# One block's signal transform with one split less, 32-row filter taps, a filter sum moved to transfers, and a new order of work

## The chip, the cores and the metric

The program runs on one core of one Trainium2 chip. The metric is device time in microseconds (us) of one execution, lower is better. The kernel before takes 259.0 us (median of three runs, 258.26 to 259.75).

The core has a matrix engine (TensorE, PE in the profile; PEld is its weight load), a vector engine (VectorE, DVE), an activation engine (ScalarE, ACT), a general engine (GpSimd, POOL) and a queue engine (SyncE, SP). They run at the same time and wait for each other through semaphores. Matrix results land in PSUM and are copied ("evicted") to SBUF by ScalarE or VectorE. Transfers are issued by SP, POOL and ACT.

## The reference, cut to what matters

```
def _A_ref(q, k, v, shift_k, ssm_k, ssm_D):        # S = 2048 tokens, D = 640
    k_shift = sum over t in 0..3 of k[s-t] * shift_k[:, t]     # per channel
    kv = k_shift * v
    y = causal convolution of kv with ssm_k along the tokens (by FFT of length 2S)
    return q * (y + kv * ssm_D)
def _B_ref(x, w_gate, w_up, w_down):               # F = 1728
    return (silu(x @ w_gate) * (x @ w_up)) @ w_down
h  = A_q + _A_ref(_layernorm(A_q), A_k, A_v, A_shift_k, A_ssm_k, A_ssm_D)
h2 = h + _B_ref(_layernorm(h), B_w_gate, B_w_up, B_w_down)
```

Everything is bfloat16 in and out.

## The kernel before, in words

The 2048 tokens are four blocks of 512, numbered 0 to 3; token 4p+j of a block lies in partition p, slot j. The long convolution is done block by block with a transform of 512 points and 256 complex frequencies, written as matrix products with cosine and sine tables (`tab`, `itab`). A block's spectrum has shape [4, 2, 640]: four groups of 64 (f), real and imaginary part, channels.

The work is a list of named tasks. A name is a kind and a block, then a part:

- `ktM.p`, `kteM.p`: transposes of filter block M on TensorE and their eviction. `kfM.fpc`, `kfeM.fpc`: filter transform by `halves` and the evictions (f half, p parity of the slots, c cosine or sine). `kbM`: its butterfly on VectorE, where `kb2.1` and `kb3.1` are accumulating transfers of POOL.
- `kcM`: sums of neighbouring filter spectra. C[1] = C[0] + R1 (`kc1`, VectorE, two halves), C[2] = R1 + K2r (`kc2.s`, one VectorE instruction on 5120 elements a partition, L687), C[3] = K2r + K3r (`kc3.0`, `kc3.1`, POOL transfers).
- `tpI.c`: the four-tap short filter of k as small matrix products with diagonal weights (L734), `keI.c` its eviction into XT (shared with the spectrum buffer XH of the same parity), `kvI.c` the product with v on VectorE (L745). Block 0 has its own path.
- `xfI`, `xfeI`, `xbI`: the signal transform, its evictions and butterflies. Block 0 uses `fulls` (groups of eight matmuls, no butterfly). `halves` splits once: eight groups of four matmuls, and two butterfly instructions of 2560 elements a partition. `quads` (set `R4X`) splits twice: eight groups of two matmuls (L622), then four butterflies of 1280 and two of 2560 (L637).
- `pJI`: product of signal spectrum J and filter spectrum C[I-J] into Y[I] (L780), in parts; those ending in `e` may be POOL accumulating transfers (L571). `p02.d` is block 2's first use of C[2], `p03` block 3's first use of C[3] and the last use of XH0.
- `ybI`, `ivI.j`: inverse butterflies and inverse transform (L922, L927). Each `ivI.j` is followed on ScalarE by an eviction `e`, a mean `m`, a square sum `s`, on VectorE by `g`, `v`, `n`, and on POOL by `r` (L840). The normalized rows go by a transposing transfer `htI.j` on SP into hnT.
- `fgI.hq`, `fuI.hq`: gate and up products of half h of the block's columns (L1032), 20 matmuls each (15 for q = 3, gate and up together). `sg`, `su`, `sv` evict them (`su` into the single buffer `ub`), `mu` multiplies (L1053). `dnI.j` is the down product (L1118; L995 for the last tile), `rsI.j` and `raI.j` add it to h (the latter an accumulating transfer), `outI.j` stores.
- `la`, `lp`: the first layer norm. `gdI.h` copies the last, half-filled gate row to the upper partitions.

Dependencies are found from the memory cells that tasks read and write, and from PSUM: the 8 banks are four units of two banks, each matmul group opens one unit, and the order plus the list `units` say which. What runs where and in which order is written out in `PLAN`: one list of task numbers for each engine. Nothing is reordered at run time: an engine that waits holds up all behind it, and so does a transfer queue that waits for its source.

Before, `KD = (3,)`, `R4X = (1,2,3)` and the taps work on 64 rows:

```
for c0 in (0, 2, 4):
    nc_ = min(2, NC5 - c0)
    pt = g.tile()
    ...
                for r in range(2):
                    rows = slice(64 * r, 64 * r + 64)
                    last = e.matmul(pt.f(r, 64 * (j1 - j0), o=256 * b + 64 * j0), ks[rows, c, k0:k0 + 509:4], ...
```

For each chunk of 128 channels that is seven shifts times two row groups of 64: 14 matmuls of 64, 128, 192 or 256 columns, 70 a block.

Of the kernel before, what the change touches and what calls it, by code (L numbers as in the profile page):

```python
# [1228 lines left out]
```

## Time and profile before

| what | value |
|---|---|
| time of the runs | 259.0 us median, 258.26 to 259.75 |
| profiled execution, its span | 256.0 us (the page gives no other time for it) |
| granted TensorE clock | 1.000 |
| matmuls | 2253 |
| TensorE / VectorE / ScalarE / GpSimd busy | 248.5 / 199.8 / 184.6 / 58.6 us |
| transfers | 35.29 MB, mean 138 GB/s |

The span is the time from the first to the last instruction. A busy time counts the span in which at least one instruction of the engine runs; matmuls overlap, so a matmul's own duration (0.27 to 0.30 us) is longer than the step from one to the next. The chain that ended last is followed back from the last instruction, at each step to what released it. Times of single tasks come from the timeline, in which each engine's instructions stand in the order of its `PLAN` list.

### The profile page before, as it was taken

How to read it: one execution, taken by the hardware profiler on the slowest of the kernel's cores; microseconds unless marked ns; L12 is line 12 of the kernel's file. 1: busy time of each engine (PE TensorE's matmuls, PEld its weight loads, DVE VectorE, ACT ScalarE, POOL GpSimd, SP SyncE). 2: the span in 40 equal slices, each digit the busy share in tenths (PEclk: the TensorE clock that was granted, in tenths of full speed). 3: DMA queues.
4: the chain of work that ended last, by engine and by line, in shares of the span. 5: the costliest groups of instructions: out<-in, count | busy, mean ns of one | idle time of the engine just before them, and what ended most of it. 6: DMA issues, size and time to landing. Idle time of an engine off the chain costs nothing.

```text
span 256.0 us, 5303 instructions
## 1 busy us (share of the span) xinstructions
PE 248.5 (97%) x2253; PEld 194.7 (76%) x2253; DVE 199.8 (78%) x256; ACT 184.6 (72%) x302; POOL 58.6 (23%) x56
## 2 busy tenths in 40 slices
PE   7999997999999999999999999999999999999995
PEld 4767773587888766888887766788886678888763
DVE  3698999999999999999999989999959534111142
ACT  2489999999996895587899789739981854526410
POOL 1001003082312053950030813334130314000000
PEclk9999999999999999999999999999999999999999
DMA  6999946787995049886956036497870142600011
GB/s 224 323 339 208 403 161 134 220 207 192 326 188 95 0 75 126 150 165 168 248 100 109 3 55 139 108 213 139 149 128 0 30 100 43 140 0 3 0 45 57
DMA packets 37620, 35.29 MB, mean 138 GB/s; under 512 B 21203, under 2 KB 32478, under 8 KB 37598
## 3 DMA queue, kind: packets, MB, share of 16 engines
q1 hardware_dynamic: 31792, 23.82, 33.2%
q0 software_dynamic: 5792, 11.14, 25.3%
q8 instruction: 17, 0.28, 0.4%
q14 instruction: 5, 0.04, 0.1%
q10 hardware_dynamic: 14, 0.01, 0.0%
HBM read 16.55 MB, written 2.62 MB: 75 GB/s over the span
## 4 chain that ended last, share of the span: by engine, by line
PE 59%; DVE 32%; DMA 4%; POOL 1%; SPq 1%; issue 1%; ACT 0%; DVEq 0%
PE ps L1032 32%; PE ps L1118 16%; DVE tt L780 9%; DVE Y L780 5%; DMA tab<-cst_tab 4%; PE ps L602 3%; PE ps L922 2%; DVE gu L1053 2%; DVE C L780 2%; DVE XH L637 2%; DVE C L564 2%; PE ps L995 2%; PE ps L622 2%; PE ps L584 2%; POOL mv L840 1%; SPq L450 1%
## 5 line engine op out<-in xcount | busy, mean ns | idle before, releaser
L1118 PE MATMUL ps<-Wd,gu 128*128 128x320 bf16 (+1 forms) x420 | 58.7, 300 | 0.0
L1118 PEld LDWEIGHTS ps<-Wd,gu 128*128 128x128 bf16 (+1 forms) x420 | 38.7, 97 | 18.4 <-issue 3.6
L780 DVE TENSOR_TENSOR tt<-XH,C 128x2560 bf16<-128x2560 bf16 (+1 forms) x31 | 47.8, 1572 | 0.6 <-ACT XH L458 0.6
L1053 DVE TENSOR_TENSOR gu<-gu,ub 128x1024 bf16<-128x1024 bf16 (+1 forms) x32 | 19.9, 621 | 26.4 <-ACT gu L1040 13.8
L1040 ACT ACTIVATE gu<-ps 128x1024 bf16<-128x1024 f32 (+1 forms) x32 | 29.4, 924 | 12.1 <-PE ps L1032 11.9
L1045 ACT ACTIVATE ub<-ps 128x1024 bf16<-128x1024 f32 x24 | 24.6, 1024 | 13.3 <-PE ps L1032 11.4
L1032 PE MATMUL ps<-hnT,GB 128*128 128x256 bf16 x280 | 34.0, 273 | 0.0
L1032 PE MATMUL ps<-hnT,UB 128*128 128x256 bf16 x280 | 33.8, 273 | 0.0
L1032 PEld LDWEIGHTS ps<-hnT,UB 128*128 128x128 bf16 x280 | 27.3, 98 | 3.4 <-ACT KO L458 0.2
L1032 PEld LDWEIGHTS ps<-hnT,GB 128*128 128x128 bf16 x280 | 27.2, 98 | 3.3
L1032 PE MATMUL ps<-hnT,GA 128*128 128x256 bf16 x240 | 28.8, 273 | 0.0
L1032 PE MATMUL ps<-hnT,UA 128*128 128x256 bf16 x240 | 28.5, 273 | 0.1
L840 POOL TENSOR_TENSOR mv<-mv,half 128x1 f32<-128x1 f32 x16 | 21.2, 1328 | 23.9 <-DVE mv L838 23.9
L1032 PEld LDWEIGHTS ps<-hnT,UA 128*128 128x128 bf16 x240 | 23.4, 98 | 3.4 <-ACT C L458 0.5
L1032 PEld LDWEIGHTS ps<-hnT,GA 128*128 128x128 bf16 x240 | 23.4, 98 | 3.2 <-DVE XH L461 0.3
L843 ACT ACTIVATE qo<-xh 128x640 bf16<-128x640 bf16 x28 | 21.0, 750 | 5.8 <-DMA xh<-in_A_q_dram 3.3
L584 PE MATMUL ps<-KT,tab 128*128 128x320 bf16 x128 | 19.8, 300 | 1.8 <-ACT K3r L458 0.7
L937 ACT ACTIVATE qo<-ps,one,st 128x640 bf16<-128x640 f32 x16 | 13.7, 887 | 9.8 <-PE ps L922 9.0
L571 POOL DMA_DIRECT2D xh<-RB x12 | 10.7, 889 | 34.4 <-DVE RB L1135 23.0
L584 PEld LDWEIGHTS ps<-KT,tab 128*128 128x128 bf16 x128 | 11.4, 98 | 8.6 <-ACT K3r L458 1.6
L840 POOL TENSOR_TENSOR st<-st,half 128x4 f32<-128x4 f32 x4 | 8.0, 1988 | 33.3 <-DVE st L835 21.5
L458 ACT ACTIVATE XH<-ps 128x640 bf16<-128x640 f32 x19 | 13.3, 736 | 1.4 <-PE ps L622 0.7
(112 smaller groups left out, 384.3 us busy)
## 6 DMA issues: line engine op xcount, KB each, us to landing
C<-US POOLq DMA_DIRECT2D x6, 640.0 KB, 6.0
kc<-in_A_ssm_k_dram SPq DMA_DIRECT2D x4, 640.0 KB, 10.3
xh<-in_A_q_dram SPq DMA_DIRECT2D x4, 640.0 KB, 5.6
out_dram<-xh SPq DMA_DIRECT2D x15, 160.0 KB, 1.9
kvo<-in_A_v_dram SPq DMA_DIRECT2D x3, 640.0 KB, 4.5
xh<-RB POOLq DMA_DIRECT2D x12, 160.0 KB, 2.9
Wd<-in_B_w_down_dram SPq DMA_DIRECT2D x1, 1280.0 KB, 7.9
C<-K3r POOLq DMA_DIRECT2D x2, 640.0 KB, 8.0
```

Source lines behind the costliest of these rows:

```text
L458: return e.activation(out=dst[1], in_=src(), func=ACTF.Copy, scale=scale)
L571: return g.add(name, "pool", lambda e, n: e.dma_start(dst, src, accum_op=ALU.add, max_dma_last_dim=4096), ("acc", 2 * int(np.prod(dst.shap ...
L584: last = e.matmul(pt.f(c, W), tab[:, f, cs, j], src[:, j, c * W:(c + 1) * W], start=(j == js[0]), stop=(j == js[1]))
L780: g.add(nm, "dve", lambda e, n_: e.tensor_tensor(out=d, in0=a, in1=b, op=op), ("sb", n * D), r=[a, b], w=[d])
L840: g.add(name + "r", "pool", lambda e, n: e.tensor_tensor(out=dst, in0=tmp, in1=hf, op=ALU.pow), ("pp", 4), r=[tmp, half[:]], w=[dst])
L843: g.add(name + "m", "act", lambda e, n: e.activation(out=junk, in_=x, func=ACTF.Identity, scale=-1.0 / D, accum_out=sm), ("aa", D, 0), r=[ ...
L937: g.add(nm + "e", "act", lambda e, n, pt=pt, q2=q2, s=s, j=j: e.activation(out=q2, in_=pt.f2(W), func=ACTF.Identity, scale=s[:, 3, j:j + 1 ...
L1032: last = e.matmul(pt.f(q // 2, 256, o=256 * (q % 2)), w[:, c, f0:f0 + P], hnT[:, c, cols], start=(c == 0), stop=(c == NC5 - 1))
L1040: g.add("sg%d.%d%d" % (i, h, gp), "act", lambda e, n, pa=pa, gv=gv, nf=nf: e.activation(out=gv, in_=pa.f(0, 256 * nf).rearrange("p (f x) - ...
L1045: g.add("su%d.%d%d" % (i, h, gp), "act", lambda e, n, pb=pb: e.activation(out=ub[:].rearrange("p b x -> p (b x)"), in_=pb.f(0, 1024), func ...
L1053: g.add("mu%d.%d%d" % (i, h, gp), "dve", lambda e, n, gv=gv, ubv=ubv: e.tensor_tensor(out=gv, in0=gv, in1=ubv, op=ALU.mult), ("sb", 256 * ...
L1118: last = e.matmul(pt.f(c, W), gu[k, fb, col(i, j)], Wd[k, fb, c * W:(c + 1) * W], start=st, stop=sp)
```

## The change

Six things change in what is computed, and the order of everything.

1. `R4X` loses block 1: `xf1` is made by `halves` instead of `quads`. Eight groups of four matmuls stand for eight of two, and `xb1` has two butterflies of 2560 instead of four of 1280 and two of 2560.
2. The taps of blocks 1 to 3 take the first four channel chunks in one task on 32 rows a matmul: 112 matmuls of 32 to 128 columns instead of 56 of 64 to 256. The task opens two PSUM units at once and has two evictions (`a`, `b`) of 1024 elements and one kv product of 2048. The fifth chunk stays on 64 rows.
3. `KD` gets block 2: `kc2` is two accumulating transfers issued by POOL (`kc2.0`, `kc2.1`), each 640 KB, instead of one VectorE instruction.
4. A task may open several PSUM units (`opens` is a list), and waits for the last users of each.
5. `KO`, the odd half of a filter transform, becomes four names at the same address. `DV`, `BNT` and `KOT` are added and empty.
6. `PLAN` is new throughout, the PSUM units with it.

```
-    KD = (3,)
+    KD = (2,3)
...
+    T32 = ((0, 4, 32), (4, 1, 64))
...
-    R4X = (1,2,3)
+    R4X = (2,3)
...
-            for c0 in (0, 2, 4):
-                nc_ = min(2, NC5 - c0)
-                pt = g.tile()
+            for c0, nc_, rr in T32 if i in KVACT else ((0, 2, 64), (2, 2, 64), (4, 1, 64)):
+                nr = P // rr
+                pts = [g.tile() for _ in range(nr // 2)]
...
-                            for r in range(2):
-                                rows = slice(64 * r, 64 * r + 64)
-                                last = e.matmul(pt.f(r, 64 * (j1 - j0), o=256 * b + 64 * j0), ks[rows, c, k0:k0 + 509:4], diag[rows, c, j0 - s:j1 - s, :],
-                                                start=(s == 0), stop=(s == -3))
+                            for r in range(nr):
+                                rows = slice(rr * r, rr * r + rr)
+                                x0 = rr * r % 64
+                                last = e.matmul(pts[r // 2].f(r % 2, rr * (j1 - j0), o=4 * rr * b + rr * j0), ks[rows, c, k0:k0 + 509:4],
+                                                diag[rows, c, j0 - s:j1 - s, x0:x0 + rr], start=(s == 0), stop=(s == -3),
+                                                **({"tile_position": (rr * r, 0)} if rr < 64 else {}))
...
-            if t.opens is not None:
-                prev = last.get(t.opens.unit)
+            for pt in t.opens:
+                prev = last.get(pt.unit)
                 if prev is not None:
-                    t.pre = {x for x in prev.users if x.eng != "pe"}
-                    t.deps.update(t.pre)
-                last[t.opens.unit] = t.opens
+                    t.pre |= {x for x in prev.users if x.eng != "pe"}
+                last[pt.unit] = pt
+            t.deps.update(t.pre)
```

The new order, with task names for the numbers, over the stretch that the prediction speaks of. TensorE:

```
kt0.0 kt0.1 xf0.00 kf0.010 kf0.000 kf0.001 kf0.011 kf0.100 kf0.101 xf0.20 kf0.110 kf0.111 kt1.1 kt1.0 xf0.21 xf0.01
kt2.0 xf0.10 xf0.30 xf0.11 xf0.31 kf1(six) tp1.4 kf1.100 kf1.000 kt3.0 tp1.0 kt2.1 iv0.0 kf2.100 kf2.000 iv0.1
kf3.000 kf3.100 kt3.1 kf2.110 kf2.011 kf2.001 kf3.101 kf2.111 kf2.101 kf2.010 iv0.3 xf1.011 xf1.100 iv0.2 xf1.001
xf1.110 xf1.010 xf1.101 kf3.001 xf1.111 xf1.000 fg0.00 kf3.010 fg0.01 kf3.111 kf3.110 kf3.011 fu0.00 fu0.01 fu0.02
fg0.03 fg0.02 fu0.10 fg0.10 fg0.12 dn0.0 fg0.11 iv1.0 dn0.0b iv1.1 fu0.11 iv1.3 fu0.12 iv1.2 fg0.13 dn0.1 dn0.2
dn0.3 fg1.00 tp2.0 tp2.4 fu1.00 fg1.02 xf2.31 ... dn1.2 xf3.01 xf3.10 iv2.3 iv2.2 xf3.11 xf3.31 dn1.3 xf3.30 xf3.21
xf3.00 xf3.20 fu2.00 ...
```

It was, from the same point: `kt0.0 kt0.1 xf0.01 xf0.00 kf0(eight) kt1.1 kt1.0 xf0.20 xf0.21 kt2.0 xf0.31 kt2.1 xf0.11 xf0.10 xf0.30 kf1(seven) kt3.0 kf1.110 tp1.2 tp1.0 iv0.0 iv0.1 tp1.4 kf2.101 iv0.2 iv0.3 kf3.001 kf2.100 kf2.111 xf1.30 xf1.31 kf2.010 ... fu0.00 xf1.20 xf1.00 fg0.00 xf1.21 fg0.01 kt3.1 kf3.100 fu0.01 kf3(six) fu0.02 fg0.11 ... dn1.3 xf3(eight) fg2.00 ...`

VectorE, from the product of block 0 on:

```
p00(eight) kv1.4 yb0.0 kb1.0 kte2.1 kb1.1 iv0.0g yb0.1 kv1.0 kfe2.110 iv0.1g iv0.0v kte3.1 kfe2.001 kc1.s2 iv0.1v
iv0.0n kc1.s0 iv0.1n kb2.0 iv0.3g xfe1.001 iv0.2g p01.a p01.b iv0.2v xb1.0 iv0.3v p01.c iv0.2n p01.d iv0.3n kb3.0
xb1.1 mu0.00 p11.0(a b c d) mu0.01 p11.0e p11.1a mu0.02 p11.1(b c d) mu0.03 p11.1e la1v gd0.0 yb1.0 p02.d yb1.1
mu0.10 iv1.0g p02.a iv1.1g p02.c iv1.0v p02.b mu0.11 ... p03.a iv1.3n p03.c kv2.4 p03.d kv2.0 ... mu1.00
```

POOL: `... kb2.1 kc2.1 iv0.2r iv0.3r kb3.1 kc2.0 kc3.1 kc3.0 la1r ra0.0 ...` (before: `kb2.1 iv0.3r iv0.2r kb3.1 kc3.1 kc3.0 la1r p02.e ...`). SP, from the loads of block 1: `kT1 itab GB v1 PKu UA GA WdC UB x1 WdB kT2 ht0.0 ht0.1 WdA ht0.2 ht0.3 ht1.1 ...` (before: `kT1 GA itab UB v1 UA kT2 PKu ht0.0 ht0.1 GB WdC x1 WdB ht0.3 ht0.2 v2 WdA ht1.0 ...`). GA, GB, UA, UB and Wd are the FFN weights; WdA overwrites the space of the filter transposes KT and waits for the last `kf3`.

More of the change, by code (lines that the diff above doesn't have):

```diff
@@ L97, in add @@
         t.pre = set()
-        t.opens = None
+        t.opens = []
         t.tiles = []
@@ L118, in add @@
             if not pt.writers:
-                t.opens = pt
+                t.opens.append(pt)
             else:
@@ L217, in emit @@
                 wait_for(t, t.pre | {x for x in t.deps if x.name == fill[0]})
-                prog["pe"].append(lambda e, t=t, fill=fill: self.filler(e, t.opens, *fill))
+                prog["pe"].append(lambda e, t=t, fill=fill: self.filler(e, t.opens[0], *fill))
             wait_for(t, t.deps)
@@ L356, in bass_sequential_preLN__ssm_conv_h3__swiglu_ffn__prompt_kernel @@
     BN = (0,)
-    BNH = ()
+    BNT = ()
+    KOT = ()
     DT = ()
@@ L411, in bass_sequential_preLN__ssm_conv_h3__swiglu_ffn__prompt_kernel @@
         v0 = sb("v0", 134400, [4, D])
-        KO = sb("KO", 143616, [2, 2, D])
+        KO = [sb("KO%d" % m, 174336 if m in KOT else 143616, [2, 2, D]) for m in range(4)]
         ub = sb("ub", 148736, [2, N])
@@ L660, in kfwd @@
             if m in R4K:
[L661 removed]
+                quads("kf%d" % m, KT[m], dst, KO[m], D ** 0.5 / N, m)
                 return
@@ L731, in mm @@
                             k0 = 16 + s
[L732 to L738 removed]
+                            for r in range(nr):
[4 more added lines that the diff above has]
+                                                **({"tile_position": (rr * r, 0)} if rr < 64 else {}))
+                    return last
+                g.add("tp%d.%d" % (i, c0), "pe", mm, ("tap%d" % rr, nc_), r=[diag[:, c0:c0 + nc_], ks[:, c0:c0 + nc_, :]], pw=pts)
+                pt = pts[0]
                 cols = slice(c0 * P, (c0 + nc_) * P)
@@ L742, in taps @@
                     ks_ = XT[i % 2][:, c0:c0 + nc_, :]
-                    evac("ke%d.%d" % (i, c0), (ks_, ks_.rearrange("p b (r y) -> p r b y", r=2)),
-                         lambda pt=pt, nc_=nc_: pt.f2(256 * nc_).rearrange("p r (b y) -> p r b y", b=nc_), N * nc_, pt)
-                    g.add("kv%d.%d" % (i, c0), "dve", lambda e, n, d=d, vv=vv, ks_=ks_: e.tensor_tensor(
-                        out=d.rearrange("p j (b x) -> p b j x", x=64), in0=ks_.rearrange("p b (r j x) -> p (b r) j x", r=2, j=4),
-                        in1=vv.rearrange("p j (b x) -> p b j x", x=64), op=ALU.mult), ("sb", N * nc_), r=[vv, ks_], w=[d])
+                    kr = ks_.rearrange("p b (r y) -> p r b y", r=nr)
+                    for h, pt in enumerate(pts):
+                        kh_ = kr[:, 2 * h:2 * h + 2]
+                        evac("ke%d.%d%s" % (i, c0, "ab"[h] if nr > 2 else ""), (kh_, kh_),
+                             lambda pt=pt, nc_=nc_, rr=rr: pt.f2(4 * rr * nc_).rearrange("p r (b y) -> p r b y", b=nc_), 8 * rr * nc_, pt)
+                    g.add("kv%d.%d" % (i, c0), "dve", lambda e, n, d=d, vv=vv, ks_=ks_, rr=rr, nr=nr: e.tensor_tensor(
+                        out=d.rearrange("p j (b x) -> p b j x", x=rr), in0=ks_.rearrange("p b (r j x) -> p (b r) j x", r=nr, j=4),
+                        in1=vv.rearrange("p j (b x) -> p b j x", x=rr), op=ALU.mult), ("sb", N * nc_), r=[vv, ks_], w=[d])
                     continue
@@ L799, in prod @@
                 op2(nm + ".d", yim, u[:, :, 0], u[:, :, 1], ALU.add, 4)
+                return
+            if (j, i) in DV:
+                x, k, re = XH[j % 2][:], cm[:], tt[:, 1].rearrange("p a b d -> p (a b) d")
+                im = US[:].rearrange("p a b c d -> p (a b) c d")
+                ksw = bass.AP(k.tensor, k.offset + D, [list(k.ap[0]), [2 * D, 4], [-D, 2], [1, D]])
+                nm = "p%d%d" % (j, i)
+                for f2 in range(2):
+                    s = slice(f2, f2 + 3, 2)
+                    op2(nm + ".%da" % f2, t1, x[:, s], k[:, s], ALU.mult, 4)
+                    op2(nm + ".%dc" % f2, re[:, s], t1[:, :, odd], t1[:, :, 1 - odd], ALU.subtract, 2)
+                addto(nm + ".0e", y[:, :, odd], re)
+                op2(nm + ".0b", im, x, ksw, ALU.mult, 8)
+                for q in range(2):
+                    addto(nm + ".%df" % q, y[:, :, 1 - odd], im[:, :, q])
                 return
@@ L973, in inverse @@
                     stats(nm, x, q[:], m[:, 0:1], m[:, 1:2])
-                rstd(nm, m[:, 1:2], m[:, 3:4], m[:, 2:3], half[:, 0:1], i in BNH or i in SA, D ** -2.0 if i in SA else float(D))
+                rstd(nm, m[:, 1:2], m[:, 3:4], m[:, 2:3], half[:, 0:1], (i, j) in BNT or i in SA, D ** -2.0 if i in SA else float(D))
                 if i in NACT:
@@ L984, in inverse @@
                 g.add(nm + "n", "dve", lambda e, n, x=x, q=q, m=m, mm_=mm_: e.tensor_scalar(
-                    out=q[:], in0=x, scalar1=mm_, scalar2=m[:, 3:4], op0=ALU.subtract if i in BNH + SA else ALU.add, op1=ALU.mult),
+                    out=q[:], in0=x, scalar1=mm_, scalar2=m[:, 3:4], op0=ALU.subtract if (i, j) in BNT or i in SA else ALU.add, op1=ALU.mult),
                       ("ts", D), r=[x, mm_, m[:, 3:4]], w=[q[:]])
```

34 lines of the change are left out of this document (15 added, 19 removed), and 53 rows, old and new, of the table PLAN.

## The prediction

> **What bounds the kernel now.** I read the page first: the busy shares, then the chain that ended last.
>
> ```profile
> PE 248.5 (97%) x2253; PEld 194.7 (76%) x2253; DVE 199.8 (78%) x256; ACT 184.6 (72%) x302; POOL 58.6 (23%) x56
> PE 59%; DVE 32%; DMA 4%; POOL 1%; SPq 1%; issue 1%; ACT 0%; DVEq 0%
> ```
>
> TensorE is busy nearly throughout, but a third of the chain is VectorE. The chain in order of time shows where it changes hands; columns are start, length, work.
>
> ```profile
> 23.62 0.56 PE ps L550 x10
> 24.18 3.27 PE ps L602 x24
> 27.47 0.71 ACT XH L458
> 28.28 2.90 DVE tt L780 x2
> ...
> 62.53 2.74 DVE C L687
> ...
> 111.64 1.55 DVE kvo L745 x3
> 113.23 0.72 PE ps L622 x4
> 113.95 2.18 PE ps L1032 x20
> ...
> 149.79 3.77 PE ps L1118 x28
> ```
>
> TensorE sets the pace to 27.5, VectorE from 28.3 to 113.2, TensorE again to the end. Two rows give streaming rates: 2.18/20 = 0.109 us for a matmul of 256 columns, 3.77/28 = 0.135 for one of 320. The windows view of the middle stretch and of the one place in it where TensorE starves:
>
> ```profile
> 28.30:109.30 81.00, 78.92 (x720) 60.11 (x720) 79.98 (x84) 71.14 (x122) 26.51 (x19) 1.00 0.71 167
> 39.82:49.23 9.41, 7.33 (x44) 3.03 (x42) 9.03 (x12) 9.41 (x18) 2.38 (x2) 1.00 0.61 129
> ```
>
> Columns are window, length, then busy PE, PEld, DVE, ACT, POOL. VectorE works 79.98 of 81.00 us. In the second window 44 matmuls of at most 0.135 us are 5.9 us in 9.41: 3.5 us are lost, with ScalarE full (9.41 of 9.41). PSUM evictions hold TensorE there. Timelines of the two engines:
>
> ```profile
> 42.51 0.72 PE L584 MATMUL ps<-KT,tab 128*128 128x320 bf16 x4 [0.69 <-ACT K3r L458]
> 43.29 0.45 PE L622 MATMUL ps<-kvo,tab 128*128 128x320 bf16 x2
> 43.88 0.44 PE L622 MATMUL ps<-kvo,tab 128*128 128x320 bf16 x2
> 44.29 0.73 ACT L458 ACTIVATE XH<-ps 128x640 bf16<-128x640 f32 x1
> 44.87 0.74 ACT L458 ACTIVATE C<-ps 128x640 bf16<-128x640 f32 x1
> ```
>
> Block 1's transform gives two matmuls (0.27 us) per eviction, and starts follow the eviction pitch, 0.58 us.
>
> **The change, part by part.**
>
> *Block 1 split once.* Eight groups of two matmuls become eight of four: 16 x 0.135 = +2.15 us of TensorE. Evictions stay eight. In the starved stretch a group may last 0.58 us at no cost and four matmuls last 0.54, so I price it at 0 there. The cover is the 3.5 us; without it the cost is the whole 2.15. VectorE loses four butterflies of 1280; rows by line and shape:
>
> ```profile
> L637 DVE TENSOR_TENSOR OS<-XH,OS 128x1280 bf16<-128x1280 bf16 x6 | 4.9, 820 | 0.2 <-ACT OS L458 0.2
> L687 DVE TENSOR_TENSOR C<-C,C 128x5120 bf16<-128x5120 bf16 x1 | 2.8, 2822 | 0.0
> L461 DVE TENSOR_SCALAR KO<-ps 128x640 bf16<-128x640 f32 x1 | 0.8, 825 | 0.4 <-PE ps L584 0.4
> L460 DVE COPY KT<-ps 128x1280 bf16<-128x1280 bf16 x1 | 0.8, 815 | 0.0
> ```
>
> Instructions overlap by 0.08, as the chain's 2.74 for L687 against 2.82 shows, so four are 4 x 0.74 = -2.96 us.
>
> *Third filter sum by transfers.* kc2 leaves VectorE (L687): -2.74. Two accumulating transfers of 640 KB enter POOL's queue: kc2.1 ahead of iv0.2r, kc2.0 between kb3.1 and kc3.1. An issue takes 1.2 to 1.7 us there:
>
> ```profile
> 66.97 1.21 POOL L571 DMA_DIRECT2D K3r<-KO  x1 [7.55 <-DVE K3r L564]
> 67.72 1.69 POOL L571 DMA_DIRECT2D C<-K3r  x1
> 74.72 1.20 POOL L571 DMA_DIRECT2D C<-K3r  x1 [5.30 <-DMA K3r<-KO]
> 77.51 1.40 POOL L840 TENSOR_TENSOR st<-st,half 128x4 f32<-128x4 f32 x1 [1.60 <-DVE st L838]
> K3r<-KO POOLq DMA_DIRECT2D x1, 640.0 KB, 7.5
> C<-K3r POOLq DMA_DIRECT2D x1, 640.0 KB, 9.9
> ```
>
> Behind kc2.1 wait iv0.2r and iv0.3r, whose inputs come some 4 us later: nothing. Behind kc2.0 and kc3.0 waits la1r; it is needed by iv1.0's eviction near 81 and I expect it near 77: nothing, with 3 to 4 us of cover. Who waits for kc2.0 itself is p02.d on VectorE. Two accumulations together took 67.72 + 9.9 - 66.97 = 10.6 us, so three (kb3.1, kc2.0, kc3.1) should take about 16.0. From the end of kb3.0 to p02.d the new VectorE order has 16.7 us (one butterfly and yb1.0, 2.8; two half products and their adds, 11.4; four gate products and small ones, 2.5). That covers it by 0.7: cost 0, ends 0 and +4.
>
> *Evictions that change engine.* The new order gives VectorE kte2.1, kte3.1, kf2.110, kf2.001 and xf1.001 between 28 and 113: 5 x 0.74 = +3.7. ScalarE loses 3 x 0.58 and two copies of about 1.1: -4.0. That shortens the stretch where ScalarE is the limit.
>
> *Early order.* Before, TensorE idles 0.37 us for the second half of the transform table, and kt2.1 (0.56, the L550 row at 23.62) stands ahead of the last group that p00.1 needs. The new order runs four groups on the first half meanwhile and puts kt2.1 later: p00.1 starts 0.93 earlier than 28.28.
>
> *VectorE's sum to the end of block 2's kv products.* -2.96 - 2.74 + 3.7 = -2.0; gd0.0 moves here, +0.2; one kv product of 2048 for two of 1024, about -0.1; p03.d (1.4) now stands before the last kv2 and mu1.00 (0.6) after it, +0.8; start, -0.93. Sum -2.0. Two new waits of about 0.1 (kv1.4 on its eviction; kte2.1): **-1.9**. So xf2's first group starts at 111.3 rather than 113.23.
>
> Does TensorE get there? fg0.00 needs the PSUM unit of xf1.101. ScalarE's list up to that eviction, from 35.3, is 14 evictions x 0.58, four inverse ones x 0.85, four statistics x 0.8: 14.8, so the unit is free at 50.2 and fg0.00 starts near 50.9 (51.97 before, where fu0.00 was already done). The 35.3 is the row at which ScalarE starts iv0.0's eviction now, 35.7, moved by the earlier start and the copies it no longer makes. From there I add groups at the two rates. To fu0.10: five of 20 matmuls (fg0.00, fg0.01, fu0.00 to fu0.02, 10.9), fg0.02 and fg0.03 (3.8), four of kf3 (2.2) with 0.1 of waits: 17.0, so 67.9. To iv1.0: fu0.10, fg0.10, fg0.12, fg0.11 (8.7) and dn0.0's first part (2.7): 79.3. To the end of fg1.02: four inverse groups (4.3), dn0.0b (1.1), two up groups and fg0.13 (6.0), three dn (11.3), three groups of block 1 (6.5), taps (1.6), 0.4 of waiting for the unit of rs0.3: 110.5, inside 111.3. So VectorE still sets the start of xf2, and TensorE's added 2.15 us is paid out of the 3.5. The margins on the way are small: mu0.01 ends near 68.6 by VectorE's sum, so `ub` is free and su0.02 done at 69.7, where fg0.10 wants the unit at 70.1; fg0.12 and dn0.0 follow with less than 0.5 us to spare. If VectorE is a microsecond late there, TensorE is late by about half of it.
>
> *32-row taps.* The first four chunks go from 56 matmuls of 64 rows to 112 of 32 rows and half the columns. The windows view, tap instructions alone, per block:
>
> ```profile
> 32.28:34.23 1.95, 1.95 (x56) 1.88 (x56) 1.00 1.06 378
> 36.51:37.09 0.58, 0.58 (x14) 0.51 (x14) 1.00 0.00 0
> 108.06:110.46 2.40, 2.40 (x70) 2.33 (x70) 1.00 0.92 153
> 138.30:140.67 2.37, 2.37 (x70) 2.30 (x68) 1.00 0.03 5
> ```
>
> 14 matmuls, 2048 columns, take 1.95/4 = 0.49 us; at 0.109 per 256 one after another they would take 0.87, so the two row groups run side by side. Four groups: 512 columns each, 0.22, plus today's 0.05 of overhead is 0.27 a chunk, 1.1 for four. No row shows a matmul of 32 rows, so I bound it: saving 0.95 (half) to costing 1.95 (today's 1.95/56 = 0.035 per matmul, times 112). I take a saving of 0.7 a block, nearer the side-by-side row. Block 1's lies in ScalarE's stretch and block 2's behind VectorE: 0 each. Block 3's is on TensorE's path: **-0.7**. The group opens two PSUM units at once; before block 3 both come from evictions that ended earlier.
>
> *After block 2.* xf3 is dealt out around dn1.3, not in one run; it loses some 0.7 us now, where 16 matmuls (2.16) fill 2.85. I take 0, between 0 and -0.5. The tail keeps its order.
>
> **The sum**: -1.9 - 0.7 = -2.6. The profiled span is 256.0, hence 253.4; the median of the runs is 259.0, 3.0 above that span, hence **256.4 us**.
>
> **Rivals.**
>
> *A. The second half of hnT comes late: slower.* In the new SP order WdA stands ahead of ht0.2 and ht0.3; before, it stood behind them.
>
> ```profile
> 57.36 0.37 SPq L450 DMA_DIRECT2D Wd<-in_B_w_down_dram  x1
> 59.40 2.96 SPq L453 DMA_TRANSPOSE hnT<-qo  x2
> 63.55 0.37 SPq L450 DMA_DIRECT2D Wd<-in_B_w_down_dram  x1
> Wd<-in_B_w_down_dram SPq DMA_DIRECT2D x1, 1280.0 KB, 7.9
> hnT<-qo SPq DMA_TRANSPOSE x16, 2.6
> xh<-RB POOLq DMA_DIRECT2D x1, 160.0 KB, 4.7
> hnT<-qo SPq DMA_TRANSPOSE x1, 4.7
> ```
>
> WdA is released by the last filter transform, near 58, and lands by 66; the transposes, issued near 59 and 61, follow at 66.5. fu0.10 reads them near 67.9 (50.9 plus 17.0 of groups). The last two rows, of the window at 95, show a transpose beside an accumulation: 4.7 instead of 2.6. If kb3.1, kc2.0 and kc3.1 (from 62) hold the transposes by the same 2.1, fu0.10 waits 0.7: 257.1. If they hold them until they land, near 78, it waits 10: 266. It decides from a landing at 72 (256.4 + 4.1 = 260.5). For it: the order; against: the transposes start before the accumulations.
>
> *B. p02.d waits for kc2.0.* Shared with WdA the trio may take 2 us more than 16.0: VectorE stops 1.3 us, xf2 starts so much later, 257.7; with 4 us, 259.7.
>
> *C. Narrow matmuls don't run four abreast.* Then block 3's taps cost +1.95, not -0.7, and block 2's as much, less 0.6 of cover: 256.4 + 2.65 + 1.35 = 260.4. Against it: the two-abreast row. The Trainium skill, TensorE: Matmul & The Clock Gate, section Wait — 56ns, not 53.3ns?, says that starts never come closer than about 25 ns however few the columns; by it 112 would take an estimated 2.8 us, +0.85 a block, about 258. The tap rows don't refute it: their mean is 35 ns.
>
> *D. TensorE recovers all of its stretch.* 3.5 us of starving and two blocks of taps at 0.7: -4.9, 254.1; VectorE would have to gain as much by meeting fewer waits.
>
> **How the numbers follow.** Forecast 0.45, A 0.20, B 0.13, C 0.10, D 0.12. 0.5% (1.3 us) is about what a measurement of this kernel can tell from no change: the bounds are 257.7 and 260.3. Faster: 0.39 of the forecast's 0.45, D, 0.03 of A: 0.54. Slower: 0.15 of A, 0.05 of C, 0.03 of B and 0.02 of the forecast: 0.25. Same: the rest, 0.21. The range goes from D's 254.0 to 261.5, which leaves out A's far end and little else; the forecast's own is 255 to 258.
>
> **What would show it.** Right: kv2's last product ends near 111.3 and xf2 starts there; taps of block 3 near 1.7 us in place of 2.37; no L687; TensorE's lost time between 36 and 51 under 2 us; fg0.00 near 51. Wrong: PE waiting on hnT before the first L1032 of the second half (A), VectorE idle before L780 at p02.d with a DMA as releaser (B), taps above 2.4 us (C), or ScalarE waiting for `ub` between 62 and 78, so that units come late for fg0.12 and dn0.0.

## The result, and the profile after

The changed kernel takes 255.59 us (median of six runs, 254.66 to 256.76), the kernel before 258.91 on the same chip: a ratio of 0.9889, 95% interval 0.9858 to 0.9920. The forecast was 256.4, in a range of 254.0 to 261.5. The profiled execution has a span of 253.1 us (before: 256.0), at a granted clock of 1.00.

The page after, first the busy shares, then the chain by engine:

```profile
PE 247.4 (98%) x2437; PEld 196.0 (77%) x2437; DVE 196.6 (78%) x252; ACT 181.6 (72%) x298; POOL 57.9 (23%) x58
PE 63%; DVE 31%; DMA 2%; POOL 1%; issue 1%; ACT 0%; DVEq 0%; POOLq 0%
```

TensorE executes 184 matmuls more, and its busy time falls by 1.1 us; the span falls by 2.9. VectorE keeps a third of the chain. The chain in order of time (start, length, work) shows that the hand-over has moved, not gone:

```profile
26.46 5.58 DMA kvo<-in_A_v_dram
...
110.29 1.15 DVE kvo L748
111.48 0.72 PE ps L619 x4
112.20 2.18 PE ps L1049 x20
...
147.30 3.77 PE ps L1135 x28
```

The first of these lines is new: VectorE's kv1.4 needs block 1's part of v, and its load was in flight for 5.58 us. The timeline of VectorE shows the wait:

```profile
32.14 0.43 DVE L748 TENSOR_TENSOR kvo<-XT,kvo 128x512 bf16<-128x512 bf16 x1 [0.49 <-DMA kvo<-in_A_v_dram]
```

In the ten other traces of the new order that load takes 3.9 to 4.5 us and kv1.4 doesn't wait. So VectorE comes some 0.5 us later here than in an execution without that wait, and differences of this size between two traces are no evidence by themselves.

The product of block 2 at line 748 (line 745 before) ends at 111.4 and the first group of xf2 starts at 111.48, against 113.23 before: 1.75 us earlier. From there to the end of the span it is 253.1 - 111.48 = 141.6 us, against 256.0 - 113.23 = 142.8: another 1.15. The middle stretch and the stretch in which TensorE starved, in the windows view (window, length, then busy PE, PEld, DVE, ACT, POOL):

```profile
28.30:109.30 81.00, 79.78 (x885) 62.85 (x883) 79.90 (x88) 69.06 (x119) 28.61 (x24) 1.00 0.83 186
38.80:48.55 9.75, 8.91 (x68) 6.07 (x67) 9.31 (x14) 9.48 (x20) 2.77 (x3) 1.00 1.07 258
```

VectorE still works 79.9 of 81.0 us. TensorE runs 68 matmuls in 9.75 us where it ran 44 in 9.41. I summed over all tasks of TensorE the step from its first matmul to the next task's, less its matmuls at the rates of the prediction (taps at their own time). These waits, from 15 us on, add up to 7.0 us before and 4.2 after: 4.0 and 2.3 of them lie between 28 and 52 us, 1.0 and 0.55 between there and 113, 1.9 and 1.3 behind that. The streaming work itself is 0.2 us more. The 0.3 us that is left of the 2.9 lies ahead of 15 us, where TensorE no longer waits for the second half of the transform table. So the gain is TensorE's waits, and the added matmuls are nearly paid by the shorter taps.

How close the two engines come at the hand-over, from their timelines:

```profile
109.08 2.35 PE L1049 MATMUL ps<-hnT,GB 128*128 128x256 bf16 x20
...
110.21 1.22 DVE L748 TENSOR_TENSOR kvo<-XT,kvo 128x2048 bf16<-128x2048 bf16 x1
...
111.48 0.72 PE L619 MATMUL ps<-kvo,tab 128*128 128x320 bf16 x4
```

fg1.02's 20 matmuls at 0.109 end at 109.08 + 2.18 = 111.26. TensorE stands 0.2 us there, no more: the first 111 us are now two sums of nearly equal length, VectorE's and TensorE's. Which of them is the longer changes from one execution to the next, since the wait of 0.49 us for v alone is more than this margin.

### The profile page after: what moved, and what is told of

It is laid out like the page before. It is cut to its first block, busy times and chain, and to the rows that moved or that the text cites. A ratio compares the mean times of both kernels' runs of the same rounds, so it can differ in the third digit from the quotient of the medians.

```text
span 253.1 us, 5668 instructions
## 1 busy us (share of the span) xinstructions
PE 247.4 (98%) x2437; PEld 196.0 (77%) x2437; DVE 196.6 (78%) x252; ACT 181.6 (72%) x298; POOL 57.9 (23%) x58
## 3 DMA queue, kind: packets, MB, share of 16 engines
q0 software_dynamic: 6336, 12.45, 28.2%
## 4 chain that ended last, share of the span: by engine, by line
PE 63%; DVE 31%; DMA 2%; POOL 1%; issue 1%; ACT 0%; DVEq 0%; POOLq 0%
PE ps L1049 32%; PE ps L1135 17%; DVE tt L783 8%; DVE Y L783 6%; PE ps L599 4%; DVE C L783 2%; DMA kvo<-in_A_v_dram 2%; PE ps L939 2%; PE ps L581 2%; DVE C L561 2%; PE ps L1012 2%; PE ps L619 2%; DVE gu L1070 2%; PE ps L732 2%; DVE US L783 1%; DVE kvo L748 1%
## 5 line engine op out<-in xcount | busy, mean ns | idle before, releaser
L1070 DVE TENSOR_TENSOR gu<-gu,ub 128x1024 bf16<-128x1024 bf16 (+1 forms) x32 | 19.9, 621 | 27.1 <-ACT ub L1062 15.1
L1057 ACT ACTIVATE gu<-ps 128x1024 bf16<-128x1024 f32 (+1 forms) x32 | 28.8, 914 | 15.3 <-PE ps L1049 15.2
L1049 PEld LDWEIGHTS ps<-hnT,UB 128*128 128x128 bf16 x280 | 27.4, 98 | 3.3
L1049 PEld LDWEIGHTS ps<-hnT,GB 128*128 128x128 bf16 x280 | 27.3, 98 | 3.3
L857 POOL TENSOR_TENSOR mv<-mv,half 128x1 f32<-128x1 f32 x16 | 16.1, 1010 | 44.3 <-DVE mv L855 44.2
L581 PEld LDWEIGHTS ps<-KT,tab 128*128 128x128 bf16 x128 | 12.2, 98 | 6.5 <-ACT K3r L455 0.8
L857 POOL TENSOR_TENSOR st<-st,half 128x4 f32<-128x4 f32 x4 | 8.7, 2165 | 29.7 <-DVE st L852 19.5
L455 ACT ACTIVATE XH<-ps 128x640 bf16<-128x640 f32 x17 | 11.9, 715 | 2.3 <-PE ps L599 1.5
```

Of the source, the lines that this page charges most:

```text
L455: return e.activation(out=dst[1], in_=src(), func=ACTF.Copy, scale=scale)
L581: last = e.matmul(pt.f(c, W), tab[:, f, cs, j], src[:, j, c * W:(c + 1) * W], start=(j == js[0]), stop=(j == js[1]))
L857: g.add(name + "r", "pool", lambda e, n: e.tensor_tensor(out=dst, in0=tmp, in1=hf, op=ALU.pow), ("pp", 4), r=[tmp, half[:]], w=[dst])
L1049: last = e.matmul(pt.f(q // 2, 256, o=256 * (q % 2)), w[:, c, f0:f0 + P], hnT[:, c, cols], start=(c == 0), stop=(c == NC5 - 1))
L1057: g.add("sg%d.%d%d" % (i, h, gp), "act", lambda e, n, pa=pa, gv=gv, nf=nf: e.activation(out=gv, in_=pa.f(0, 256 * nf).rearrange("p (f x) - ...
L1070: g.add("mu%d.%d%d" % (i, h, gp), "dve", lambda e, n, gv=gv, ubv=ubv: e.tensor_tensor(out=gv, in0=gv, in1=ubv, op=ALU.mult), ("sb", 256 * ...
```

## The experiments

Theory **V**: up to xf2 the time is the longer of two sums. VectorE's ends with kv2.0 (111.4), TensorE's 0.2 us before. What is put on VectorE in that stretch shows in full; what is put on TensorE costs what exceeds its waits; and the evictions on VectorE pay for ScalarE's stretch. The rivals, each told in the expectations, are that the order alone, TensorE's waits alone, ScalarE's stretch, or the transfers make the time. Every kernel was timed against the kernel before on the same chip. The table has the median and ratio, and from the profiled execution the start of p00.1 (it lies between 27.1 and 28.1 in the eleven executions of the new order and moves what follows), the start of xf2, and TensorE's time from there to its last matmul.

| kernel | us | ratio, 95% interval | p00.1 | xf2 | xf2 to end |
|---|---|---|---|---|---|
| changed kernel | 255.59 | 0.9889 [0.9858, 0.9920] | 27.3 | 111.5 | 139.0 |
| u_taps | 256.90 | 0.9943 [0.9920, 0.9967] | 27.7 | 112.6 | 140.0 |
| u_kc2 | 258.46 | 1.0003 [0.9981, 1.0025] | 27.4 | 113.7 | 139.0 |
| u_quads | 259.24 | 1.0036 [1.0015, 1.0057] | 27.6 | 115.6 | 139.2 |
| new_order | 262.78 | 1.0180 [1.0140, 1.0221] | 27.3 | 118.5 | 139.6 |
| u_quads_split | 259.06 | 1.0031 [1.0001, 1.0060] | 27.1 | 114.0 | 139.0 |
| ev_act | 260.33 | 1.0083 [1.0057, 1.0110] | 27.5 | 116.0 | 139.0 |
| old_order | 260.14 | 1.0076 [1.0053, 1.0099] | 28.2 | 115.0 | 140.4 |
| old_order_kf3 | 261.42 | 1.0110 [1.0078, 1.0141] | 28.4 | 116.4 | 140.1 |
| kv2_first | 256.16 | 0.9910 [0.9881, 0.9939] | 27.4 | 111.2 | 139.7 |
| yb_early | 255.70 | 0.9877 [0.9834, 0.9920] | 27.6 | 111.9 | 139.0 |
| tuned | 255.93 | 0.9892 [0.9858, 0.9925] | 28.1 | 111.6 | 139.7 |
| tuned2 | 256.12 | 0.9904 [0.9874, 0.9933] | 28.1 | 111.5 | 140.1 |

Beside these kernels, on their chips, the kernel before had medians of 258.91 (changed kernel), 258.27 (the next four), 258.15 (u_quads_split, ev_act, old_order and kv2_first) and 258.61 us (the rest). Differences of medians across these groups are therefore uncertain by half a us and more.

**One part undone at a time, the new order kept.** u_taps:

```diff
-    T32 = ((0, 4, 32), (4, 1, 64))
+    T32 = ((0, 2, 64), (2, 2, 64), (4, 1, 64))
```

> The changed kernel with 64-row taps in blocks 1 to 3, all else and the order kept. Theory V (VectorE's sum paces the kernel up to xf2, TensorE after it, and TensorE's added work is paid from its waits): block 3's taps cost 0.6 us on TensorE's path, block 2's about 0.4 because fg1.02 ends only 0.2 us before xf2 can start, block 1's nothing: 1.0 us slower than the changed kernel, 256.6. Theory O (the new order of transfers and evictions brings the gain, the parts are hidden): 255.6. Theory P (TensorE's work paces everywhere): three times 0.65, 257.5.

Measured 256.90, 1.3 us above the changed kernel. In the profiled execution, the longest of the 12 runs (257.59), xf2 starts 1.1 later (0.7, if the later start of p00.1 is taken off), and the rest is 1.0 longer. The windows view of the changed kernel, tap instructions alone, for the first four chunks of block 1, then all five chunks of blocks 2 and 3:

```profile
31.90:33.25 1.35, 1.30 (x112) 1.20 (x112) 1.00 1.06 373
104.00:111.40 7.40, 1.88 (x126) 1.72 (x126) 1.00 0.91 158
132.00:134.30 2.30, 1.86 (x126) 1.81 (x126) 1.00 0.03 7
```

To the next task's start block 1's 112 matmuls take 1.24 us, 0.011 each (the 1.30 holds the drain of the last). Blocks 2 and 3 take 1.88 and 1.86 for 2.40 and 2.37 of before: 0.5 a block. With the 64-row form fg1.02 ends at 112.4, 1.1 later than in the changed kernel and 0.7 counted from p00.1: block 2's half us, which the margin of 0.2 could not hide. But VectorE's product ends at 112.5 in this execution, behind a wait of 0.44 for POOL that the changed kernel's has not at this place, so this trace doesn't tell which of the two made xf2 late. The medians speak for the taps: of 1.3 us block 3's are 0.6.

u_kc2:

```diff
-    KD = (2,3)
+    KD = (3,)
 VectorE: ... iv0.3n
+    kc2.s
     kb3.0 xb1.1 mu0.00 ...
 POOL:
-    kc2.1 (behind kb2.1), kc2.0 (behind kb3.1)
```

> The changed kernel with kc2 on VectorE again (one instruction ahead of kb3.0), without its two transfers. Theory V: VectorE has 2.74 us more ahead of kv2.0, so xf2's first group moves from 111.5 to about 114 and the time to 258.1. Theory O: 255.6, since kc2's result is not needed for 15 us. Theory P: 255.6.

258.46, 2.9 above; the eight of its 12 runs with a mean clock of 1.0 took 258.1 on average, 2.5 above. From the start of kv1.4 (31.65, and 32.14 in the changed kernel behind the wait for v) to xf2 it takes 82.08 us instead of 79.34: 2.74 more, the instruction's whole length. How it reaches TensorE is seen in the timelines of u_kc2; the last bracket is the idle time before and who ended it:

```profile
60.08 2.82 DVE L681 TENSOR_TENSOR C<-C,C 128x5120 bf16<-128x5120 bf16 x1
...
70.49 0.69 DVE L1067 TENSOR_TENSOR gu<-gu,ub 128x1024 bf16<-128x1024 bf16 x1
...
71.21 1.02 ACT L1059 ACTIVATE ub<-ps 128x1024 bf16<-128x1024 f32 x1 [1.32 <-DVE gu L1067]
...
72.29 2.36 PE L1046 MATMUL ps<-hnT,GA 128*128 128x256 bf16 x20 [2.09 <-ACT ub L1059]
```

VectorE's product mu0.01 (at 68.25 in the changed kernel) comes at 70.49; ScalarE's eviction su0.02 waits for `ub` that it reads, and fg0.10 for the PSUM unit that this eviction frees. TensorE stands 2.09 us, and xf2 starts 2.25 later.

u_quads, and new_order (all three parts undone, so the computation of before in the new order):

```diff
-    R4X = (2,3)
+    R4X = (1,2,3)
 VectorE:
-    xb1.0
+    xb1.1 xb1.0 xb1.2 xb1.3
-    xb1.1
+    xb1.4 xb1.5
```

> The changed kernel with block 1's transform split twice again, all else kept. Theory V: VectorE has four instructions of 0.74 us more, TensorE 2.15 us less; xf2's first group moves to about 114.2 and the time to 258.2. Theory P (TensorE's work paces): 2 us faster, 253.5. Theory O: 255.6.

> The new order with the old content: 64-row taps, kc2 on VectorE, block 1 split twice. Theory V: VectorE carries 5.7 us more than in the changed kernel, and 3.7 us more evictions than in the kernel before; xf2's first group moves to about 117, block 3's taps cost 0.6: 261.8, slower than the kernel before. Theory O: the order alone brings the gain, about 256.

Measured 259.24 and 262.78, each about 1 us more than V expected. The undone parts add up roughly: 1.3 + 2.9 + 3.6 = 7.8 for the single ones, 7.2 for all three. The rival that the order alone makes the gain falls: by itself it is 1.8% slower than the kernel before, with a mean clock of 0.993 or less in all six of its runs. The missing microsecond is in the same place as u_kc2's wait. u_quads, first the timeline, then the windows view of these matmuls, in which the number behind the POOL count is the granted clock:

```profile
73.05 3.90 PE L1046 MATMUL ps<-hnT,GA 128*128 128x256 bf16 x20 [2.52 <-ACT ub L1059]
```

```profile
73.05:76.74 3.69, 3.69 (x20) 2.71 (x21) 3.65 (x4) 3.61 (x8) 1.20 (x1) 0.58 1.08 192
```

The 20 matmuls behind a wait of 2.52 us take 3.69 us instead of 2.18, at a granted clock of 0.58. Of u_quads' 12 runs six had a mean clock of 1.0 and took 258.7 on average, six had 0.993 and took 259.8.

u_quads_split asks whether the length of that one wait is what costs the clock. It is u_quads with fu0.10 held back so that a part of the wait comes ahead of it:

```diff
         for name, fill in self.fills.items():
             byname[name].deps.add(byname[fill[0]])
+        byname["fu0.10"].deps.add(byname["p11.0b"])
```

> The changed kernel with block 1 split twice again (as u_quads), and one wait more: fu0.10 on TensorE waits for p11.0b on VectorE, about 1.7 us after it could start. Nothing else is changed. Theory K (TensorE's idle time of 2.5 us ahead of fg0.10 halves its granted clock for 3.4 us, which costs 1.5 us): the idle time falls into two shorter ones, the clock stays at 1.0, and the kernel is 1.5 us faster than u_quads, 257.7, though it only waits more. Rival (the group ran slowly for another reason, or its time is hidden): 259.2 or more.

The timeline of TensorE in its profiled execution:

```profile
69.45 2.36 PE L1047 MATMUL ps<-hnT,UA 128*128 128x256 bf16 x20 [2.04 <-DVE tt L781]
72.57 2.36 PE L1047 MATMUL ps<-hnT,GA 128*128 128x256 bf16 x20 [0.77 <-ACT ub L1060]
```

In the profiled execution the clock stays at 1.0 and the span is 1.8 us shorter than that of u_quads, with xf2 at 114.0. But the median is 259.06: six of the 12 runs had a mean clock of 0.993 and took 259.4, six 0.999 or 1.0 and took 258.4. So a fall costs about 1 us, but splitting the wait into 2.04 and 0.77 did not make it rarer, and K's 257.7 did not come.

What decides it can be read from the clock records of the traces. A stretch of full or half clock, up to the kernel's end, always lasts a whole number of steps of 3.413 us (64.85, 3.41 and 180.91 us in u_quads, 249.17 in u_kc2). So the clock changes only at the borders of such steps, and where they lie differs from one execution to the next. The windows view of single steps: in u_quads the one that holds the wait and the one behind it, then the emptiest of u_quads_split and of u_kc2:

```profile
70.25:73.66 3.41, 0.89 (x9) 0.56 (x7) 3.38 (x5) 2.09 (x3) 0.23 (x1) 1.00 1.07 194
73.66:77.07 3.41, 3.41 (x18) 2.42 (x17) 3.41 (x4) 3.33 (x8) 0.96 (x1) 0.50 1.06 190
65.91:69.32 3.41, 1.50 (x14) 1.09 (x12) 3.41 (x5) 2.66 (x5) 1.12 (x1) 1.00 1.08 187
68.46:71.87 3.41, 1.74 (x16) 1.31 (x14) 3.41 (x5) 2.06 (x4) 1.20 (x1) 1.00 1.09 194
```

The number behind the length is TensorE's busy time. In all 14 traces the clock is halved behind each step with 1.37 us of it or less (0.9 in u_quads and new_order, 0.98 in ev_act, the others at the kernel's end), and behind none with 1.49 or more. So a wait of 2.5 us costs the clock when it falls into one step, and not when two share it. new_order shows both: its wait of 2.49 ahead of 70.56 lies across a border at 69.0 and costs nothing, that of 2.52 ahead of 75.43 lies in the step from 72.41 to 75.82, behind which the clock is halved. That the runs without a trace fell in this way is not shown.

Without the fall the undone butterflies cost 2.8 to 3.1 us, near the 2.96 of the prediction.

**The evictions.** ev_act puts the five back on ScalarE:

```diff
 VectorE:
-    kte2.1 kf2e.110 kte3.1 kf2e.001 xf1e.001
 ScalarE: ke1.0b
+    kte2.1
 ... kf2e.000
+    kte3.1
 ... iv0.0s
+    kf2e.110
 ... kf2e.011
+    kf2e.001
 ... iv0.2e
+    xf1e.001
```

> The changed kernel with the five evictions kte2.1, kte3.1, kf2.110, kf2.001 and xf1.001 on ScalarE instead of VectorE, at places where their matmuls have just ended. Theory V: VectorE has 3.7 us less, but ScalarE 4.0 more in the stretch where it limits TensorE; fg0.00 moves from 51.5 to about 54.5, and the time by about 3: 258.6. Rival (VectorE alone paces up to xf2): faster, down to 252.

260.33, 1.7 above V's figure and on the other side from the rival. At these places ScalarE's lateness costs more than VectorE's 3.7 us are worth; other places were not tried. The longest of its waits in the timeline of ev_act, and the windows view of the stretch that begins with it:

```profile
41.81 0.72 PE L579 MATMUL ps<-KT,tab 128*128 128x320 bf16 x4 [2.10 <-ACT qo L952]
```

```profile
41.81:45.20 3.39, 2.65 (x11) 1.18 (x12) 1.77 (x3) 3.39 (x8) 1.06 (x1) 0.65 1.25 263
```

TensorE stands 2.1 us for an eviction queued behind the copies, and its clock falls here too (0.65; 11 of 12 runs had a mean of 0.993 or less). fg0.00 starts at 55.6 instead of 51.4, and VectorE itself waits 5.3 us for ScalarE's statistics. With all three parts undone (new_order) fg0.00 starts at 50.6: what TensorE gains between 28 and 52 us hangs on the moved evictions, not on the three parts.

**The parts without the order.** old_order has the new computation in the order, on the engines and in the PSUM units of before; where a task has no counterpart it stands where the last of the old ones stood:

```diff
 TensorE: xf1.30 xf1.31 xf1.11 ... -> xf1.011 xf1.111 xf1.110 ...; tp2.2 tp2.0 -> tp2.0
 VectorE:
-    xb1.0 xb1.1 xb1.2 xb1.3 xb1.4 xb1.5 kc2.s
+    xb1.0 xb1.1
 POOL:
+    kc2.1 (behind kb2.1), kc2.0 (behind kb3.1)
```

> The new content (32-row taps, kc2 by transfers, block 1 split once) in the order, engines and PSUM units of the kernel before; kc2.1 stands behind kb2.1 and kc2.0 behind kb3.1 on POOL. Theory V: VectorE has 5.7 us less, so kv2 could end near 107.5, but ScalarE still has all evictions and TensorE the 2.15 us more: fg1.02 ends near 112.8, xf2 starts 0.4 earlier than 113.24, block 3's taps save 0.6: 257.9. Theory W (the content alone brings the gain): 255.6.

260.14: slower than before, where V expected 257.9. V as stated fails here, since VectorE's sum shrank by 5.7 us and nothing came of it. The timeline of VectorE, before:

```profile
61.04 1.49 DVE L637 TENSOR_TENSOR XH<-OS,XH 128x2560 bf16<-128x2560 bf16 x1
62.44 2.82 DVE L687 TENSOR_TENSOR C<-C,C 128x5120 bf16<-128x5120 bf16 x1
65.18 1.49 DVE L564 TENSOR_TENSOR K3r<-K3r,KO 128x2560 bf16<-128x2560 bf16 x1
```

and in old_order, with the windows view of the gap:

```profile
59.94 1.48 DVE L558 TENSOR_TENSOR XH<-XH,OS 128x2560 bf16<-128x2560 bf16 x1
65.03 1.49 DVE L558 TENSOR_TENSOR K3r<-K3r,KO 128x2560 bf16<-128x2560 bf16 x1 [3.60 <-ACT KO L452]
```

```profile
61.43:65.03 3.60, 3.60 (x30) 2.59 (x29) 0.00 (x1) 3.60 (x7) 0.00 (x0) 1.00 1.20 268
```

kb3.0 starts where it started, 65.0, because it needs the last kf3 group, which TensorE reaches at 63.3 and ScalarE evicts by 65.0, both busy throughout. VectorE's spared instructions have become this wait of 3.6 us and one of 1.5 at 55.5, also for ScalarE, which the kernel before has not. Behind it kb3.0 to the end of block 2's product takes 49.9 us against 48.0, with waits for ScalarE of 0.9 and 0.6 and 0.3 for the accumulations; and TensorE waits 1.3 us for the second half of hnT, whose transposes lie in flight together with kc2.1 and three loads.

The last step asks whether K3r's evictions are the whole of it: the kf3 groups ahead of fu0.01, and three of their evictions on VectorE.

```diff
 TensorE: fg0.01 kt3.1
-    kf3.100 fu0.01 kf3.101 kf3.000 kf3.111 kf3.110 kf3.011 kf3.010
+    kf3.100 kf3.101 kf3.000 kf3.111 kf3.110 kf3.011 kf3.010 fu0.01
 ScalarE -> VectorE: kf3e.100 kf3e.101 kf3e.111
```

> The kernel old_order (new content, old order, 260.1) with kf3.x ahead of fu0.01 on TensorE, and three of the kf3 evictions on VectorE, where it stood 3.6 us waiting for ScalarE ahead of kb3.0. Theory V (old_order is slow because the work that VectorE is spared comes back as a wait for K3r's evictions): kb3.0 starts at 62.5 to 63.2 instead of 65.03 and two thirds of that reach the end, 258.5 (257.9 to 259.2). Rival W (the transfers set it: TensorE's 1.4 us wait for the second half of hnT ahead of fg0.11, and the trio of accumulations ahead of p02.d at 84.2): 259.8 or more, with fg0.11 still at 67.3 or later.

261.42. The edit did not do what it should: kb3.0 starts at 65.5. VectorE and TensorE in its timeline:

```profile
61.70 1.48 DVE L558 TENSOR_TENSOR XH<-XH,OS 128x2560 bf16<-128x2560 bf16 x1
63.10 0.82 DVE L455 TENSOR_SCALAR KO<-ps 128x640 bf16<-128x640 f32 x1
63.97 0.72 PE L578 MATMUL ps<-KT,tab 128*128 128x320 bf16 x4 [0.87 <-DVE KO L455]
...
65.46 1.49 DVE L558 TENSOR_TENSOR K3r<-K3r,KO 128x2560 bf16<-128x2560 bf16 x1 [1.55 <-ACT KO L452]
```

The evictions stand on VectorE behind a butterfly of 1.48, so their PSUM units come late and TensorE waits for them in turn; hnT is no longer waited for, and yet the time grew. That the transfers alone make old_order slow is not supported, and that K3r's evictions alone make it slow is not shown either.

**Is there a reserve?** Four orders of the changed kernel, each with one or two places moved on VectorE:

```diff
 kv2_first:  p03.c kv2.4
+    kv2.0
     p03.d
-    kv2.0
 yb_early:   kb1.0 kte2.1
+    yb0.1 iv0.0g
     kb1.1
-    iv0.0g yb0.1
 tuned:      both
 tuned2:     tuned, and mu1.01, mu1.02, mu1.03 ahead of xb2.1, xb2.2, xb2.4
```

> The changed kernel with kv2.0 ahead of p03.d on VectorE. Theory V: kv2.0 ends 1.4 us earlier, but TensorE ends fg1.02 only 0.2 us before xf2 starts now, so 0.2 is gained: 255.4. Rival (VectorE alone holds xf2): 1.4 is gained, 254.2.

> The changed kernel with one VectorE addition of block 0 (yb0.1) moved ahead of kb1.1 and of the eviction addition iv0.0g, so that TensorE no longer stands 1.2 us at 39 to 41 us. Theory V (two sums pace the kernel up to the first xf2: VectorE's, ending at 111.4 with kv2.0, and TensorE's, 0.2 us behind): VectorE's sum is unchanged, so the first xf2 still starts at 111.3 to 111.6 and the time stays within 0.3 us of the changed kernel, 255.4. Rival T (TensorE alone paces, each wait taken away counts): 254.4, the first xf2 at 110.3.

> yb0.1 moved as in yb_early, and kv2.0 ahead of p03.d, so that both sums up to the first xf2 end earlier (VectorE's by 0.85 us as in kv2_first, TensorE's by up to 1.2). Theory V: the first xf2 at 110.5 to 110.7. Then p03.d and what is behind it on VectorE stand 0.4 to 0.7 us later against TensorE (in kv2_first mu1.01 came 0.67 us later and TensorE lost 0.6 before tp3.4): 255.4 if that loss stays 0.6, 254.8 if it does not come. Rival: the multiplications mu1.x pace and not kv2.0, no gain over kv2_first: 256.2.

> The edits of tuned, and mu1.01, mu1.02 and mu1.03 each one or two places earlier on VectorE, ahead of xb2.1, xb2.2 and xb2.4, so that the evictions of the second feed-forward on ScalarE do not wait for them. If the loss of 0.6 us before tp3.4 came from mu1.x: 254.8 with no wait ahead of tp3.4. If it did not: as tuned. Above 255.8 the later xb2.x delay p22 and the inverse transform of block 2.

256.16, 255.70, 255.93 and 256.12: none differs from the changed kernel by more than its interval. yb_early takes only 0.4 of the 1.2 us off TensorE's wait at 39 to 41, as the groups there then wait for KO's eviction; that leaves too small a step in the time to tell T from V. Its trace speaks for V: fg1.02 ends at 111.22, and xf2 still waits until 111.84 for VectorE's product, which ends at 111.79. In tuned xf2 follows p00.1 by 83.5 us instead of 84.2; 0.5 of these 0.7 is the changed kernel's wait for v, so the order won little up to there, and the stretch behind it is 0.7 longer. The place is shown by the timelines, first kv2_first's, then tuned2's:

```profile
133.15 1.31 PE L729 MATMUL ps<-diag,kT 32*128 32x128 bf16 x112 [0.47 <-ACT gu L1054]
```

```profile
147.20 1.26 PE L936 MATMUL ps<-Y,itab 128*128 128x320 bf16 x8 [0.72 <-DVE Y L648]
```

With kv2.0 first the mu1 products come later, ScalarE's evictions with them, and TensorE waits at tp3. With the mu1 products moved up as well that wait is gone, and VectorE is late for the inverse transform of block 2 instead. In the changed kernel VectorE works 33.6 of the 34.0 us from 113 to 147 as well; these orders only chose where TensorE meets it.

## Why the prediction was right, step by step

- **VectorE's sum, -1.9**: measured -1.75 (xf2 at 111.48 for 111.3). The parts that runs could single out fit: without the clock's fall four butterflies 2.8 to 3.1 (2.96) and kc2 2.5 by the runs, 2.74 by the trace (2.74); p00.1 1.0 earlier in this execution, 0.75 on the average of the eleven of the new order (0.93). One term was missed: the two new waits were put at 0.1, and kv1.4 alone stood 0.49, for the load of v and not for its eviction. As the other traces don't have that wait, it is partly luck that the sum met 111.3 so closely.
- **Added matmuls of block 1 at 0, fg0.00 near 50.9**: xf1's groups follow each other at 0.54 us, TensorE's own rate, and the kernel paid 0.2 us of streaming for all of its changes. fg0.00 starts at 51.44: 0.5 late, by two waits of kf2 groups (0.48 and 0.36) that the working did not have. The reason given, that a group of two already lasted an eviction's pitch, was half of it: ev_act shows that the cover exists only because five evictions left ScalarE. The prediction's sum has them only as a cost on VectorE (+3.7); what ScalarE is spared (-4.0) stands in the working of fg0.00 and not in the sum. Undone they cost 4.7 us, the clock's fall included.
- **kc2 by transfers at 0**: right, with more room than estimated. The timeline of POOL and VectorE, and then the transfers issued from 62 to 64.5 (the last number is the time from issue to landing):

```profile
62.35 1.21 POOL L568 DMA_DIRECT2D K3r<-KO  x1 [3.40 <-DVE K3r L561]
63.10 1.70 POOL L568 DMA_DIRECT2D C<-C  x1
63.83 2.20 POOL L568 DMA_DIRECT2D C<-K3r  x1
...
77.44 1.49 DVE L561 TENSOR_TENSOR OS<-Y 128x2560 bf16<-128x2560 bf16 x1
78.85 1.48 DVE L783 TENSOR_TENSOR tt<-XH,C 128x2560 bf16<-128x2560 bf16 x1
```

```profile
K3r<-KO POOLq DMA_DIRECT2D x1, 640.0 KB, 7.1
C<-C POOLq DMA_DIRECT2D x1, 640.0 KB, 9.5
C<-K3r POOLq DMA_DIRECT2D x1, 640.0 KB, 12.9
```

  The three take 63.83 + 12.9 - 62.35 = 14.4 us (estimate: 16.0). kc2.0 itself lands at 63.10 + 9.5 = 72.6, and p02.d starts at 78.85 right behind yb1.0: rival B had 6 us against it.
- **Rival A, the second half of hnT**: it didn't come. The timeline of SP's queue with TensorE's reader, and the two transfers by issue:

```profile
58.17 0.38 SPq L447 DMA_DIRECT2D Wd<-in_B_w_down_dram  x1
58.92 3.73 SPq L450 DMA_TRANSPOSE hnT<-qo  x2
...
68.35 2.35 PE L1049 MATMUL ps<-hnT,UA 128*128 128x256 bf16 x20
```

```profile
Wd<-in_B_w_down_dram SPq DMA_DIRECT2D x1, 1280.0 KB, 7.0
...
hnT<-qo SPq DMA_TRANSPOSE x2, 6.1
```

  WdA lands at 65.2, the transposes at 66.0 and 66.5, 1.8 us before they are read. Beside loads and accumulations the two transposes took 6.1 us in the mean (7.0 and 5.2); they started before the trio, as the prediction argued.
- **Taps, -0.7 for block 3, 0 for block 2**: the four chunks saved what was forecast, 1.95 - 1.24 = 0.71 in block 1 (0.31 a chunk, where 0.27 was added up and a margin left). A whole block saves less, 0.53 and 0.58 from its first matmul to the next task's (2.40 to 1.87 in block 2, 2.38 to 1.79 in block 3): the fifth chunk, 0.48 as a fifth of such a run, takes 0.63 and 0.55 now that it stands by itself. And block 2's half us counts in TensorE's sum, because fg1.02 ended at 111.26 and not at 110.5. Rival C falls. The Trainium skill, TensorE: Matmul & The Clock Gate, section Wait — 56ns, not 53.3ns?, has no start closer than about 25 ns; these 112 matmuls start 0.011 us apart on average. Taken for each of the four row groups by itself that is 0.044 apart, which the rule allows; taken for the engine, the measurement contradicts it.
- **After block 2 at 0**: that stretch gained 1.15, of which the taps are 0.5. The rest is TensorE's waits, 0.4 less from 113 to 160 and 0.2 less behind it; which of the moves made them shorter was not tried.
- **The total**: the profiled span is 253.1 for 253.4. The other 0.5 of the distance between 256.4 and 255.6 is that the median stands 2.5 above this profiled span, and was taken as 3.0.
- **Rival D** (254.1) asked for all of TensorE's waits in the stretch; 1.7 of 4.0 went.

The four combinations in one view: computation and order of before 258.9; new computation alone 260.1; new order alone 262.8; both 255.6. No part has a gain of its own that could be added up from the kernel before. The forecast came out because it was summed along the new order of each engine, not part by part.

## What to carry to other kernels

Where two engines run full side by side, cost a change along the new order of each engine and compare the two sums at the place where they meet; the margin there (here 0.2 us, less than one load varies between executions) says whether the next saving will show. Work taken off an engine can be worth nothing until its next input comes earlier too: look up who releases the instruction behind the one removed. And where evictions hold TensorE, moving a few to the engine that seems to be the bound can be worth more than they cost there.
